# Two more turns for the DMA engines: q and k from the third batch on, A from the fourth, with a re-planned schedule

## The chip, the cores and the metric

The kernel runs on one core of a Trainium2 chip. The metric is the device time of one execution in microseconds (us). Before the change it was 260.49 us, the median of three runs (260.13 to 261.2). The profiled execution of it took 260.93 us, and the span of its instructions in the profile is 258.8 us; all times within the profile are counted from the start of that span.

The engines are named as the profile names them: PE is the matrix engine (PEld its weight loads), DVE the vector engine, ACT the scalar engine, POOL the general one (GpSimd), and SP the engine that does nothing here but issue DMAs.

## What is computed

The reference is Nystromformer attention over 8 batches of 8 heads, 576 positions and 64 features, followed by an MLP with a squared ReLU over the 4608 resulting rows of 512 features. Cut to what matters:

```python
q_lm = q.reshape(B, H, 32, 18, D).mean(axis=3)     # 32 landmarks, each a mean of 18 rows
k_lm = k.reshape(B, H, 32, 18, D).mean(axis=3)
A  = softmax(scale * q    @ k_lm.T)                # 576 x 32
Bm = softmax(scale * q_lm @ k_lm.T)                # 32 x 32
C  = softmax(scale * q_lm @ k.T)                   # 32 x 576
Z  = Bm.T / (norm1(Bm) * norminf(Bm) + 1e-6)
for _ in range(6):
    Z = 2 * Z - Z @ Bm @ Z                         # an approximate inverse
attn = A @ Z @ C @ v                               # per batch and head
h = attn_as_rows @ w_in                            # 4608 x 512 @ 512 x 2048
out = relu(h) ** 2 @ w_out                         # @ 2048 x 512
```

Inputs and output are float32; inside, the matrix engine works on bfloat16.

## The kernel before

**The work of one batch.** k, q and v come from device memory by DMAs that POOL issues (`load`, line 132; the first k by SP), cast to bfloat16 on the way except for that k. A batch's 576 rows lie as 4 blocks of 128 rows and a tail of 64 rows (`qkt` for k and q, `vt` for v). For the first three batches k and q are put into `stage`, which borrows a buffer of the MLP's; later ones use two buffers called `raw`. `prepare` (line 277) copies them on DVE into the order that the matmuls want (`nat`, line 280). From `nat`, PE forms the landmark means (`segment_means`, lines 341 and 351). The scores need k and q with the features on the partitions, so `nat` must be turned into `T` (`kT` and `qT`), and the tails into `tT`. Then come the landmark scores (line 371), the small Newton iteration for the inverse (line 413), the exponentials of A and C (`EA`, `EC`, lines 529 to 564), the sums and the scaling of A's rows into `an` (lines 571 to 583), and the turn of `an` into `AT`, with the 32 landmarks of four heads on the partitions.

The product of the rest is folded into the first weight matrix: `G` (line 806, cast on line 703) is Z C v times w_in. With it the MLP's first layer is a single product, `h` = AT x G (line 823), whose ReLU is taken by ACT (line 827) and squared by DVE into `gT` (line 828). The second layer is line 852: 36 output tiles of 128 rows, each of 16 matmuls of 512 columns, copied out on line 861 or 863 and sent off by a DMA (line 834 issues it). The last tile is made in two halves of 256 columns; the first goes out by DVE and SP, the second by ACT.

**Turning, on two engines.** A turn on PE (`transposed`, line 312; `transposed_tail`, line 322; `a_transposed`, line 596) multiplies by the identity into PSUM and is copied out by DVE or ACT (lines 662, 664, 685; 730 and 747 in the head). From batch `DMA_T` on, `prepare` instead lets SP issue a DMA that transposes (lines 285 and 286), and from batch `DMA_A` on `a_transposed` does the same (line 590). Before the change these are 3 and 4 (batches are counted from 0). `load_qk` makes the k and q loads of batch b wait for the DMA turns of batch b-1, and the k load also for the turns of A of batch b-2.

**The order of work.** For PE, DVE, ACT and SP it is written out by hand. `HEAD` is the order for the attention of batch 0. Then `PLANS[b]` interleaves, for each b, the 16 `h` and 16 squarings `s` of batch b's first layer, the attention steps of batch b+1 (a `+` behind a token puts it to batch b+2), and as many matmuls of the second layer as a number says, taken from one running generator over all output tiles. The tokens that matter here:

- `pk`, `pq`: prepare k or q; `tk0 tk1 tq0 tq1 tt`: turn on PE and copy out (they do nothing in a plan where DMAs turn, and are left out there)
- `mk`, `mq`, `lm`: means of k and of q, landmark scores; `ls ib if jo jl nu nn wt`: softmax and inverse
- `sk0 sk1 sq0 sq1 tl`: scores and exponentials against kT, qT and tT; `as ar at`: sums, rows and turn of A; `cv`: C v
- `gg0`, `gg1` (and `g:1` to `g:3` for batch 0): G; `w:n` in the head: n matmuls on zeros while PE waits for data

Every engine takes its instructions strictly in that order, so an instruction that waits holds up all behind it on its engine. POOL's DMAs run in the order of `LOADS` and then batch by batch (`load_next`).

Of the kernel before, what the change touches and what calls it, by code (L numbers as in the profile page):

```python
# [9 lines left out]
P = 128  # L10
# [5 lines left out]
F32 = mybir.dt.float32  # L16

B = 8
H = 8
# [5 lines left out]
DM = 512  # L25
# [3 lines left out]
TAIL = S - NC4 * P  # L29
HALF = S // 2  # L30
SCALE = 1.0 / 8.0
DMA_T = 3
DMA_A = 4
DMA_C = 9
COMPACT = 1
HEAD = (
    "w:16 ck tk1 tk0 ek0a w:1 ek1d w:1:256 cq0 w:1 mk cq1 w:1 tt mq et tq0 eq0a tq1 lm eq1d "
    "ls tl sum:0:4:5 sq1 ib sum:1:0:2 sk0 if w:1:256 sq0 w:1 sum:1:2:5 jo rec:1 sk1 "
    "sum:0:0:2 w:1:256 jo row:1:0:3 w:1:256 sum:0:2:4 w:1:256 jo cv:0 cv:1 rec:0 cr w:1 "
    "row:1:3:5 cba jo ct w:1:256 row:0:0:3 at:1 row:0:3:5 jl at:0 ea1a w:1 ea0d nu g:0 gf1a "  # L40
    "fv gf0d az gl0d w:1 gl1a"
)
LOADS = "v0 w10 w00 q1 w11 w01 o0 o1 v1 o2 o3"
PLANS = [
    (
        "pk h tt h g:1 s pq s tk1 h h tk0 tq1 h mk s s mq h s tq0 lm h h ls ib if sk0 s g:2 s jo "
        "g:3 tl h jo 2 sq0 s jo h s 1 as0 jl sq1 h h 1 ar0 nu sk1 s s h nn 1 h as1 1 s nu cv nn1 "
        "h s h wt 2 ar1 at0 gg1 s 1 s s 1 at1 2 gg0"
    ),
    (  # L50
        "6 h 1 s 5 h pk 2 h tt h 1 s 1 s 2 h 1 mk pq 1 mq tq0 1 h s 1 lm tq1 2 tl 1 s 1 h h 1 "
        "sq0 s 1 ls 1 ib if s 3 s 1 sq1 jo as1 h 3 tk0 2 pq+ 1 h jo h 1 tk1 1 s jo h 2 s 1 as0 1 "
        "jl 2 sk0 h 2 ar1 nu 3 s 1 nn sk1 1 ar0 1 h nu pk+ cv s 1 nn1 s 1 s 2 h 1 h wt 2 s at0 1 "
        "gg0 1 at1 1 s 2 gg1"
    ),
    (
        "mk 1 mq 1 h 3 lm 3 h s h ls sk1 2 ib 1 s h h s 1 s if s 2 tl 3 h 3 pk+ jo 1 sq1 3 h s s "
        "1 h sq0 jo s h as0 1 h jo 5 h s 1 h 1 as1 pq+ s jl 1 s 3 h h 1 sk0 nu 4 ar0 1 s ar1 s 4 "
        "cv nn 6 nu 3 at0 h 1 nn1 1 h s 4 wt 6 gg1 s 4 at1 s gg0 5"
    ),  # L60
    (
        "2 mk h 1 mq 3 h 1 lm 2 s 1 h 1 ls sk1 4 ib s 1 sq1 1 h 1 if pq+ 3 tl 1 jo 1 as1 3 pk+ 2 "
        "s h h 3 s s 1 s jo ar1 1 sq0 h 4 jo 4 s 2 jl as0 1 sk0 h 1 h s s 1 h 3 h nu s 1 h 1 s h "
        "nn cv ar0 h 3 nu s at0 1 at1 s h nn1 h s 3 wt s 4 s 3 gg0 5 gg1"
    ),
    (
        "mk 2 mq 9 lm 2 ls 1 h tl ib h 1 s 1 h 1 sq1 h 7 s 3 if h s 1 pq+ 1 h sq0 s s h jo 3 s s "
        "h as1 2 jo 6 h s 4 jo as0 1 h 1 pk+ 1 h 1 s jl 3 s 3 sk1 ar1 h 3 nu 3 sk0 1 ar0 1 s 1 "
        "nn at1 s 2 h nu h 1 nn1 cv h 1 s s 2 at0 s wt 1 h s 4 gg1 5 gg0"
    ),  # L70
    (
        "3 mk mq 6 lm 1 ls 2 ib 1 h s h sq0 2 h 3 if sq1 h 1 s s 2 jo h s pk+ 2 sk1 jo 1 h s 1 h "
        "s tl jo 4 s h 1 as0 h 1 ar0 4 jl 1 s sk0 h 1 h nu as1 s 4 h 2 s nn 2 at0 s 1 h nu ar1 3 "
        "s h cv nn1 s h s 1 at1 h 2 wt 1 s s 1 pq+ 3 gg0 7 gg1 3"
    ),
    (
        "mk h 1 s 7 mq h 1 h lm 2 h 1 sk1 4 s 2 ls ib if 3 s tl 1 s h 1 jo s h 1 s 1 sk0 jo 1 h "
        "1 cv h s 2 h 2 jo 1 sq0 1 h 2 as0 2 s 1 jl h s s h 1 ar0 s nu 4 sq1 h h 1 as1 4 nn 1 "
        "ar1 3 s nu 3 h 1 nn1 s 5 s s wt h 4 gg1 at1 s 5 gg0 at0 2"
    ),  # L80
    (
        "6 h 1 s 6 h 1 h s s 5 h 3 h 1 h s s 1 h s 2 h 4 s 3 h 2 h 1 s 1 s 3 h 2 h s 1 h 1 s 1 s "
        "1 h 1 h 1 s 8 h 1 s 4 s 5 s"
    ),
]

# [2 lines left out]
def kernel(  # L89
# [18 lines left out]
    psum = ctx.enter_context(tc.tile_pool(name="psum", bufs=1, space=bass.MemoryType.PSUM))  # L108

    w_in_bf = wpool.tile([P, DM // P, DFF], BF16, name="w_in_bf")  # L110
    w_out_bf = wpool.tile([P, NF, DM], BF16, name="w_out_bf")
# [44 lines left out]
    def load_qk(b: int, X: dict):  # L156

        X["qkt"] = loads.tile([P, H, D], BF16, tag="qkt", name="qkt")

        def tails():  # L160
            for src, r0 in ((k, k_row(b)), (q, q_row(b))):
                load(X["qkt"][r0:r0 + TAIL, :, :],
                     src[b, :, NC4 * P:S, :].rearrange("h p d -> p h d"))

        if b > 0:
            tails()
        for nm, src in (("k", k), ("q", q)):
            if b < 3:
                X[nm + "raw"] = staged(b, nm)
            else:  # L170
                X[nm + "raw"] = loads.tile([P, H, NC4, D], BF16, tag="raw", name="raw")
            parts = ((0, H // 2), (H // 2, H)) if b == 0 and nm == "q" else ((0, H),)
            for lo, hi in parts:
                one = load(
                    X[nm + "raw"][:, lo:hi, :, :],
                    src[b, lo:hi, 0:NC4 * P, :].rearrange("h (p c) d -> p h c d", c=NC4),
                    nc.sync if b == 0 and nm == "k" else nc.gpsimd)
                turns = [] if b == 0 else [loaded[b - 1].get(nm + "turn")]
                if b > 1 and nm == "k":
                    turns += loaded[b - 2].get("aturn", [])  # L180
                for turn in turns:
                    if turn is not None:
                        tc.add_manual_dep(
                            one.ins, turn.ins.name,
                            mybir.DependencyInfo(mybir.DependencyClass.Sync,
                                                 mybir.DependencyReason.DATA),
                            reason="behind the turning of the batch before")
            if b == 0 and nm == "k":
                tails()
# [43 lines left out]
    for i in range(2):  # L233
        ct = const.tile([P, 2, NC4 + 1, P], BF16, name="ct%d" % i)
# [62 lines left out]
    def attention(b: int, R: dict):  # L297
# [32 lines left out]
        def segment_means(ti, nm):  # L330
# [3 lines left out]
            means = both_means[ti]  # L334
            order = [(p, c) for p in range(NPAIR) for c in range(NC4 + first)]
            if first:
                order.sort(key=lambda x: (x[0] // 2, x[1] // 2, x) if nm == "q" else
                           (0, x[1] // 2, x))
            for n, (p, c) in enumerate(order):
                src = X[nm][:, c, 2 * p:2 * p + 2, :] if c < NC4 else X["qkt"][:, 2 * p:2 * p + 2, :]  # L340
# [3 lines left out]
                    rhs=seg[:, c + (ti if c == NC4 else 0), :],  # L344
# [151 lines left out]
        ct = cts[b % 2] if b >= DMA_C else None  # L496
# [212 lines left out]
        def head_step(token):  # L709
# [10 lines left out]
                st["qraw"] = natural(0, "q")  # L720
                X["tT"] = attn.tile([P, NPAIR, P], BF16, tag="tT", name="tT")
            elif name[:2] == "cq":
                lo = slice(4 * i, 4 * i + 4)
                dve(X["q"][:, :, lo, :], st["qraw"][:, :, lo, :])
            elif name[:2] in ("tk", "tq"):
                st["e" + name[1:]] = transposed(name[1], i)
# [103 lines left out]
    leaving = []  # L830
# [5 lines left out]
    def mlp_out(b, gT):  # L836

        b0 = b - b % 2
        for t in range(0, NC4) if b % 2 == 0 else range(NC4, 9):
            first, final = (b, t) == (0, 0), (b, t) == (B - 1, 8)  # L840
            if final:
                halves = [psum.tile([P, 2, DM], F32, tag="h", bufs=2, name="ops2")[:, 0, 0:DM // 2]
                          for i in range(2)]
            elif (b // 2 + t) % 2:
                halves = [ntile([P, DM], place=2)[:]]
            else:
                halves = [psum.tile([P, DM], F32, tag="o", bufs=1, name="ops")[:]]
            o_sb = mlp.tile([P, DM], F32, tag="o", bufs=3, name="o_sb")
            n = DM // len(halves)
            for i, ops in enumerate(halves):  # L850
                for f in range(NF):
                    nc.tensor.matmul(ops, lhsT=gT[:, f, t * P:t * P + P],  # L852
                                     rhs=w_out_bf[:, f, i * n:i * n + n],
                                     start=(f == 0), stop=(f == NF - 1))
                    if f == 2:
                        leave()
                    if f < NF - 1:
                        yield
                o_h = o_sb[:, i * n:i * n + n]
                if final and i == 0:  # L860
                    nc.vector.tensor_copy(o_h, ops)  # L861
                else:
                    nc.scalar.copy(o_h, ops)  # L863
                queue = nc.sync if final and i == 0 else nc.scalar
                if t == NC4:
                    for e in range(2):
                        r0 = (b0 + e) * S + NC4 * P
                        leaving.append(partial(queue.dma_start, out[r0:r0 + TAIL, :],
                                               o_h[64 * e:64 * e + TAIL, :]))
                else:  # L870
                    bb, c = (b0, t) if t < NC4 else (b0 + 1, t - NC4 - 1)
                    rows = out[bb * S:bb * S + NC4 * P, :].rearrange("(p c) n -> p c n", c=NC4)
                    leaving.append(partial(queue.dma_start, rows[:, c, i * n:i * n + n], o_h))
                if b == B - 1:
                    leave()
                yield
# [98 lines left out]
```

The softmax here doesn't subtract the row's maximum and nothing guards it: scores larger than these inputs give would overflow.

## Time and profile before

| | |
|---|---|
| Time, median of 3 runs | 260.49 us |
| Span in the profile | 258.8 us |
| Granted clock of PE | 0.998 of full speed |
| Moved by DMA | 35.96 MB, mean 139 GB/s |
| POOL's DMA queue q0 | 17.83 MB, 54.6% of the 16 engines' span |
| SP's queue q1 (first k, all turns) | 8.39 MB, 19.6% |
| ACT's queue q10 (outputs) | 9.31 MB, 10.4% |
| h matmuls (line 823), all 512 | 4 in 0.49 us of PE's stream |
| output matmuls (line 852), 560 of 512 columns | 16 in 3.45 us |

The page counts the busy time of each engine. On PE a matmul's duration reaches into the next one, so for PE the distance from one start to the next is read as well. The second part of the page cuts the span into 40 slices of 6.5 us and gives the busy share of each in tenths. The chain of waits follows the work that ended last back to what released it. DMA issues are listed with the median time from issue to landing.

### The profile page before, as it was taken

The page shows a single profiled execution, that of the slowest core. Times are in us where ns is not written, and L with a number is a line of the kernel's source. Part 1 is how long each engine was busy: PE and PEld are TensorE (multiplying, and loading weights), DVE is VectorE, ACT ScalarE, POOL GpSimd, SP SyncE. Part 2 cuts the span into 40 slices and gives each one's busy share as a digit, 9 for nine tenths or more (in the row PEclk, how much of TensorE's full clock was granted, in tenths as well). Part 3 has the DMA queues.
Part 4 walks back from the last instruction along what each step waited for, and adds up shares of the span by engine and source line. Part 5 has one row for each costly group of instructions (what it writes and reads, how often), then busy time and mean ns, then how long its engine had stood idle before and what let it go on. Part 6 is the DMA issues. An engine that isn't in the chain of part 4 may idle for free.

```text
span 258.8 us, 6890 instructions
## 1 busy us (share of the span) xinstructions
PE 250.1 (97%) x2832; PEld 150.7 (58%) x2832; DVE 174.9 (68%) x483; ACT 156.7 (61%) x275; POOL 45.5 (18%) x70
## 2 busy tenths in 40 slices
PE   7888899999999999999999999999999999999994
PEld 2655756576656655666646655566556654655453
DVE  5796899678987784588764877688857687243000
ACT  2657897677577754666756555586557655566110
POOL 8934335120024013200042002500000000000000
PEclk9999999999999999999999999999999999999999
DMA  8999999996669999959159988999351113111222
GB/s 190 180 199 204 207 200 196 193 209 122 137 104 179 209 181 168 171 113 188 35 98 199 197 196 124 148 223 176 100 123 43 43 41 91 43 42 72 52 81 81
DMA packets 75167, 35.96 MB, mean 139 GB/s; under 512 B 42752, under 2 KB 69632, under 8 KB 75136
## 3 DMA queue, kind: packets, MB, share of 16 engines
q0 software_dynamic: 39808, 17.83, 54.6%
q1 hardware_dynamic: 30080, 8.39, 19.6%
q10 hardware_dynamic: 5248, 9.31, 10.4%
q8 instruction: 22, 0.36, 0.5%
q14 instruction: 9, 0.07, 0.1%
HBM read 36.70 MB, written 9.44 MB: 178 GB/s over the span
## 4 chain that ended last, share of the span: by engine, by line
PE 86%; DMA 6%; POOL 4%; DVE 2%; issue 0%; ACT 0%; POOLq 0%; DVEq 0%
PE ops L852 26%; PE h L823 23%; PE n L852 23%; DMA stage<-in_q_dram 6%; PE g L806 3%; PE n L529 3%; PE n L341 2%; PE n L413 1%; PE n L614 1%; POOL qkt L134 1%; PE n L312 1%; PE n L629 1%; POOL stage L134 1%; PE n L596 1%; PE n L557 1%; POOL seg L205 1%
## 5 line engine op out<-in xcount | busy, mean ns | idle before, releaser
L827 ACT ACTIVATE r<-h 128x576 bf16<-128x576 f32 x128 | 81.9, 651 | 42.8 <-PE h L823 32.8
L852 PE MATMUL ops<-w_out_bf,gT 128*128 128x512 bf16 (+1 forms) x320 | 82.5, 368 | 0.0
L852 PEld LDWEIGHTS <-gT 128*128 128x128 bf16 x592 | 53.1, 97 | 39.9 <-issue 4.2
L852 PE MATMUL n<-w_out_bf,gT 128*128 128x512 bf16 x272 | 72.1, 379 | 0.0
L823 PE MATMUL h<-AT,G 128*128 128x288 bf16 x448 | 71.5, 286 | 0.0
L828 DVE TENSOR_TENSOR gT<-r 128x576 bf16<-128x576 bf16 x128 | 55.2, 449 | 19.4 <-ACT r L827 19.0
L823 PEld LDWEIGHTS <-G 128*128 128x128 bf16 x512 | 47.3, 98 | 22.3 <-DVE AZ L796 0.3
L703 DVE CAST G<-g 128x1024 bf16<-128x1024 f32 x14 | 17.1, 1222 | 6.6 <-PE g L806 6.6
L134 POOL DMA_DIRECT2D raw<-in_k_dram x5 | 4.4, 888 | 80.3 <-DMA AT<-an 23.5
L703 ACT CAST G<-g 128x1024 bf16<-128x1024 f32 x14 | 14.2, 1012 | 7.1 <-PE g L806 7.1
L863 ACT COPY o_sb<-ops 128x512 f32<-128x512 f32 (+1 forms) x19 | 10.9, 573 | 12.1 <-PE ops L852 9.0
L863 ACT COPY o_sb<-n 128x512 f32<-128x512 f32 x17 | 10.0, 587 | 8.5 <-PE n L852 8.5
L529 PEld LDWEIGHTS <-T 128*128 128x128 bf16 x256 | 11.4, 98 | 4.4 <-ACT T L730 0.5
L571 DVE TENSOR_REDUCE ra<-EA 128x20 f32<-128x640 f32 (+3 forms) x19 | 13.3, 698 | 0.6 <-ACT EA L534 0.6
L583 DVE TENSOR_TENSOR an<-EA,rra 128x640 bf16<-128x640 f32 (+2 forms) x18 | 13.1, 734 | 0.0
L529 PE MATMUL n<-bd,T 128*128 128x64 bf16 x256 | 12.8, 193 | 0.3 <-ACT T L730 0.3
L534 ACT ACTIVATE EC<-n 128x512 bf16<-128x512 f32 x16 | 9.6, 599 | 5.8 <-PE n L529 5.7
L534 ACT ACTIVATE EA<-n 128x512 f32<-128x512 f32 x16 | 9.6, 599 | 2.7 <-PE n L529 2.6
L294 PE MATMUL idle<-bd 128*128 128x512 bf16 (+1 forms) x29 | 9.3, 434 | 1.5 <-DVE bd L117 1.5
L823 PE MATMUL h<-AZ,G 128*128 128x288 bf16 x64 | 9.8, 286 | 0.1
L341 PEld LDWEIGHTS <-nat 128*128 128x128 bf16 x256 | 8.2, 96 | 2.7 <-issue 0.5
L861 DVE COPY o_sb<-ops 128x256 f32<-128x256 f32 x1 | 0.4, 425 | 13.6 <-PE ops L852 13.6
(144 smaller groups left out, 278.9 us busy)
## 6 DMA issues: line engine op xcount, KB each, us to landing
out_dram<-o_sb ACTq DMA_DIRECT2D x31, 256.0 KB, 2.9
vm<-in_v_dram POOLq DMA_DIRECT2D x8, 512.0 KB, 12.0
raw<-in_k_dram POOLq DMA_DIRECT2D x5, 512.0 KB, 6.7
raw<-in_q_dram POOLq DMA_DIRECT2D x5, 512.0 KB, 9.6
w_in_bf<-in_moe_w_in_dram POOLq DMA_DIRECT2D x4, 512.0 KB, 12.3
w_out_bf<-in_moe_w_out_dram POOLq DMA_DIRECT2D x4, 512.0 KB, 17.0
out_dram<-o_sb ACTq DMA_DIRECT2D x9, 128.0 KB, 3.5
stage<-in_k_dram SPq DMA_DIRECT2D x1, 1024.0 KB
```

Of the source, the lines that this page charges most:

```text
L134: d = queue.dma_start(dst, src)
L341: nc.tensor.matmul(means[:, ti, p, :], lhsT=src.rearrange("p h d -> p (h d)"), rhs=seg[:, c + (ti if c == NC4 else 0), :], start=(n == 0 a ...
L529: nc.tensor.matmul(sc[:, c, j, :, :], lhsT=X[nm + "T"][:, c, p, :], rhs=BD[:, 1 if nm == "q" else 0, p, 0:64], start=True, stop=True)
L534: nc.scalar.activation(dst, sc.rearrange("p c j i m -> p c (j i m)"), AF.Exp, scale=SCALE)
L571: nc.vector.reduce_sum(ra[:, quads, lo:hi, :], EA[:, quads, lo:hi, :].rearrange("p q c (h m) -> p q c h m", m=M), axis=AX.X)
L583: on.tensor_tensor(an[:, i, lo:hi, :].rearrange("p c (h m) -> p c h m", m=M), EA[:, i, lo:hi, :].rearrange("p c (h m) -> p c h m", m=M), r ...
L703: (act, dve)[n % 2](G[:, :, n * 512:n * 512 + 512], gg[:])
L823: nc.tensor.matmul(h[:, j, 0:HALF], lhsT=G[:, qd, f * P:(f + 1) * P], rhs=AT[:, qd, a0 + j * HALF:a0 + (j + 1) * HALF], start=(qd == 0), s ...
L827: nc.scalar.activation(r.rearrange("p (j t) -> p j t", j=2), h[:, :, 0:HALF], AF.Relu)
L828: return lambda: nc.vector.tensor_tensor(gT[:, f, o:o + S], r[:], r[:], ALU.mult)
L852: nc.tensor.matmul(ops, lhsT=gT[:, f, t * P:t * P + P], rhs=w_out_bf[:, f, i * n:i * n + n], start=(f == 0), stop=(f == NF - 1))
L863: nc.scalar.copy(o_h, ops)
```

## The change

`DMA_T` goes from 3 to 2 and `DMA_A` from 4 to 3: the third batch's k and q with their tails, and the fourth batch's A, are turned by DMAs instead of PE. It is meant to take this work from PE and the copies from DVE and ACT.

The first batch's q is loaded as 6 heads and 2 heads, not as 4 and 4, so that what is left to cast after the last landing is less; the order of its mean matmuls follows that. Of the weights, the half `w00` is loaded ahead of the first v instead of behind it.

The last output tile is cut in 384 and 128 columns, not in two halves, so that the copy and the DMA behind the last matmul are smaller.

`HEAD` and all of `PLANS` are written anew for this. The number of h, squarings and output matmuls in all is the same; 7 output matmuls more than before are in plan 0 (19, not 12) and 12 more in plan 1 (79, not 67), so that fewer are left for the end. In plan 0 the two casts for batch 2 (`pk+`, `pq+`) now stand at the end; before, they stood in plan 1.

```diff
-DMA_T = 3
-DMA_A = 4
+DMA_T = 2
+DMA_A = 3
 HEAD = (
-    "w:16 ck tk1 tk0 ek0a w:1 ek1d w:1:256 cq0 w:1 mk cq1 w:1 tt mq et tq0 eq0a tq1 lm eq1d "
...
+    "w:16 ck tk0 w:1:256 w:1 ek0a cq0 w:1 w:1 cq1 tk1 ek1a mk tt mq tq1 lm tq0 et eq0a eq1d "
...
-LOADS = "v0 w10 w00 q1 w11 w01 o0 o1 v1 o2 o3"
+LOADS = "w00 v0 w10 q1 w11 w01 o0 o1 v1 o2 o3"
 PLANS = [
     (
-        "pk h tt h g:1 s pq s tk1 h h tk0 tq1 h mk s s mq h s tq0 lm h h ls ib if sk0 s g:2 s jo "
-        "g:3 tl h jo 2 sq0 s jo h s 1 as0 jl sq1 h h 1 ar0 nu sk1 s s h nn 1 h as1 1 s nu cv nn1 "
-        "h s h wt 2 ar1 at0 gg1 s 1 s s 1 at1 2 gg0"
+        "h h pk tt h s s g:1 tk0 h h mk pq s s mq tq0 lm ls tq1 h s ib h if tk1 h jo g:2 jo s "
+        "sq1 g:3 jo s h s tl 1 jl as1 s h h nu 1 sq0 1 s h ar1 nn 1 sk1 1 s h sk0 as0 s nu h h s "
+        "nn1 cv s 1 h wt at1 2 ar0 gg1 s 1 s 1 at0 1 gg0 6 pk+ 2 pq+"
     ),
     (
-        "6 h 1 s 5 h pk 2 h tt h 1 s 1 s 2 h 1 mk pq 1 mq tq0 1 h s 1 lm tq1 2 tl 1 s 1 h h 1 "
-        "sq0 s 1 ls 1 ib if s 3 s 1 sq1 jo as1 h 3 tk0 2 pq+ 1 h jo h 1 tk1 1 s jo h 2 s 1 as0 1 "
-        "jl 2 sk0 h 2 ar1 nu 3 s 1 nn sk1 1 ar0 1 h nu pk+ cv s 1 nn1 s 1 s 2 h 1 h wt 2 s at0 1 "
-        "gg0 1 at1 1 s 2 gg1"
+        "6 h 3 s h 1 h 1 mk s 5 h 1 mq 1 h 2 lm s s ls h 1 h 1 s h ib 2 if tl s 2 s s h 2 jo s 1 "
+        "h 4 h jo 1 h 1 s 2 jo 1 sk1 s h 3 jl 1 h s 1 s nu 1 sk0 h 4 s nn cv nu h 1 s 1 s 1 sq1 "
+        "nn1 3 as1 4 ar1 sq0 pk+ 2 wt 2 as0 4 ar0 at1 2 gg0 7 at0 4 gg1 pq+"
     ),
...
-            parts = ((0, H // 2), (H // 2, H)) if b == 0 and nm == "q" else ((0, H),)
+            parts = ((0, 6), (6, H)) if b == 0 and nm == "q" else ((0, H),)
...
-                order.sort(key=lambda x: (x[0] // 2, x[1] // 2, x) if nm == "q" else
+                order.sort(key=lambda x: (x[0] // 3, x[1] // 2, x) if nm == "q" else
...
-                lo = slice(4 * i, 4 * i + 4)
+                lo = slice(6, H) if i else slice(0, 6)
...
-                halves = [psum.tile([P, 2, DM], F32, tag="h", bufs=2, name="ops2")[:, 0, 0:DM // 2]
-                          for i in range(2)]
+                halves = [psum.tile([P, 2, DM], F32, tag="h", bufs=2, name="ops2")[:, 0, 0:w]
+                          for w in (3 * DM // 4, DM // 4)]
```

The other six plans are reordered in the same way.

## The prediction

> **What bounds the kernel now.** I read the page's engine totals and slices, then busy time by stretch, then TensorE's (PE's) timeline around the work the change moves, then the DMA landings.
>
> ```profile
> PE 250.1 (97%) x2832; PEld 150.7 (58%) x2832; DVE 174.9 (68%) x483; ACT 156.7 (61%) x275; POOL 45.5 (18%) x70
> ...
> PE   7888899999999999999999999999999999999994
> ...
> DMA  8999999996669999959159988999351113111222
> ```
>
> PE is below 9 only in the first five slices (6.5 us each) and the last; the DMA engines are full for nine slices, to about 58 us. Matmuls overlap, so 97% alone proves little. The stretches say more (from:to, us, PE busy, matmuls, clock, DMA share, over 1 where packets overlap, and GB/s):
>
> ```profile
> 22.00:34.00 12.00, 10.55 (x165) 1.00 1.23 207
> 34.00:46.00 12.00, 12.00 (x219) 1.00 1.46 197
> 46.00:76.00 30.00, 30.00 (x370) 1.00 1.05 160
> 76.00:105.00 29.00, 29.00 (x319) 1.00 1.20 173
> ```
>
> PE idles 1.45 us between 22 and 34 us, where batch 0's MLP runs, and not at all later. The start-to-start distances agree: after 50 us they sit at the spacing of their kind (16 output matmuls in 3.45 us, 0.216 each; four h matmuls in 0.49; eight transposes in 0.45). So after 34 us the end is set by the sum of PE's work: what leaves PE there leaves the time, and what delays PE there adds to it. Before 34 us PE waits for data; the chain of waits shows for what:
>
> ```profile
> 11.75 14.59 DMA stage<-in_q_dram
> 26.36 0.70 DVE nat L280
> 27.11 0.62 PE n L312 x8
> ```
>
> Batch 1's q lands at 26.34, 14.59 us after its issue. PE's timeline (start, us, ..., count) shows the work that is to leave, each with the next start behind it:
>
> ```profile
> 53.82 0.61 PE L312 MATMUL n<-ident_bf,nat 128*128 128x128 bf16 x8
> 54.27 0.38 PE L852 MATMUL ops<-w_out_bf,gT 128*128 128x512 bf16 x1
> ...
> 97.96 0.44 PE L596 MATMUL n<-ident_bf,an 128*128 128x128 bf16 x5
> 98.24 0.65 PE L823 MATMUL h<-AT,G 128*128 128x288 bf16 x4
> ```
>
> The duration column (0.61) is longer than the place taken (53.82 to 54.27, 0.45), as matmuls overlap. The DMA issues (name, queue, count, median us to landing):
>
> ```profile
> T<-nat SPq DMA_TRANSPOSE x10, 5.3
> AT<-an SPq DMA_TRANSPOSE x8, 3.9
> ...
> tT<-qkt SPq DMA_TRANSPOSE x5, 2.8
> ```
>
> **What the Trainium skill says.** "Trainium Kernel Development and Optimization" (Performance Expectations) calls matmul busy time a bad measure, as matmuls are pipelined; the trace agrees (0.38 us long, 0.216 apart), hence the distances. "VectorE: DVE Perf Modes" (The three transpose paths) gives 390 ns for a 128x128 transpose on TensorE and 1309 ns on the DMA; in this trace a PE transpose takes 0.055 us of PE's stream, and a DMA turn of 16 blocks lands in 5.3, 0.33 a block. So the DMA is slower and pays only by leaving PE alone. "TensorE: Matmul & The Clock Gate" (PE-mode transpose) says the result goes to PSUM and needs a copy out; the trace has them, 0.69 us on VectorE (DVE), 1.01 on ScalarE (ACT). "DMA: Bandwidth & Descriptors" (Issuing engines are not separate DMA queues) says DMAs of all issuers interleave on the same 16 engines; the trace agrees: the T turns land in 4.4 to 8.8 us, the 8.8 at 85 us with loads and outputs in flight.
>
> **The change part by part.** *Off PE.* Batch 2's k and q: 4 groups of 8 transposes, at 53.82, 55.29, 61.03 and 63.38, of 0.45, 0.45, 0.44, 0.44 = 1.78 us. Its tails: 4 at 50.41, 0.22. Batch 3's A: 2 groups of 5 (from 97.96), 0.28 each, 0.56. All lie after 34 us, so they count in full: **-2.56 us**. Their copies (T 0.69 and 1.01 twice each, tT 0.42, AT 0.45 and 0.64) leave DVE and ACT, 68% and 61% busy: 0 on the path.
>
> *Onto the DMA.* One tail turn and two T turns near 46 to 60 us, two AT turns near 96. Queue q1 moved 8.39 MB in 19.6% of 258.8 us, 6.0 us per MB; so the first three (0.13 + 2 x 0.52 MB) cost about 7 us of the 16 engines, in a stretch where they are full to 58. Estimated positions in the new plans, with each token at its measured place in PE's stream (h 0.49, one output matmul 0.216, g pair 0.56, scores 0.23, means 0.40 and 0.51), plan 0 starting at 22.0 as before and losing the same 1.45 to waits: plan 1 starts at 45.7. The casts `pk+` and `pq+` stand at the end of plan 0, at 45.3 and 45.7. Their data was issued at 33.2 and 35.7; staged loads land in 13.2 (median) to 14.6, so at 46.4 to 47.8 and 48.9 to 50.3; with 0.69 for a cast they are done by 48.5 and 51.0. PE wants them for `mk` at 49.5 and `mq` at 51.7: 0.7 us of room at worst. Queued behind the waiting DVE are the squares; r has three buffers and h two, so PE notices at the sixth h, at 53.2, a good us after the casts are done. The turns then go out at 48.5 and 51.0 and land, at 5.3 to 8.8, by 57.3 and 59.8; wanted for `sk1` at 61.2 and `sq1` at 67.3. `tl` wants the tail at 55.8; issued near 46, landed by 52. All hidden: **0**.
>
> *Held loads.* With DMA_T = 2 batch 3's k and q wait for batch 2's turns: not issued at 44.6 and 45.5 but near 57 and 60. Raw loads take 6.7 and 9.6 (medians): 64 and 70. `pk+` and `pq+` for batch 3 stand near 69 and 75. Behind them on GpSimd's queue is batch 4's k (75.9 before), due again only after batch 3's k turn, near 76. Batch 5's loads now wait also for batch 3's AT turns: issued near 96 and 97, landed by 102 (3.9, 4.7 at most), while the first h that reads AT stands near 107, and batch 5's casts come after 118: **0**.
>
> *The head and plan 0.* q in 6 and 2 heads leaves a shorter cast behind the last landing (4 heads took 0.49; a quarter of q about 0.25); v behind a weight load arrives some 2.5 us later, near 15.5, against its first use at 16.4. But batch 1's q bounds what follows, so the head itself: 0. After that landing the old plan runs `tq1`, an h, `mk`, `mq`, an h, `tq0` and only then `lm` (27.11 to 29.97); the new one does `mk` ahead of it and then `mq tq0 lm`: about 28.2. The latency chain of batch 1 starts 1.8 us sooner, with five h before the landing, not four. What this can win is between 0 and the 1.45 idle; I take half: **-0.7 us**.
>
> *Last tile.*
>
> ```profile
> 255.23 0.37 ACT L863 COPY o_sb<-ops 128x256 f32<-128x256 f32 x1 [2.91 <-PE ops L852]
> 255.64 0.34 ACTq L834 DMA_DIRECT2D out_dram<-o_sb  x1
> ```
>
> PE: 32 x 0.109 = 3.49 becomes 16 x 0.162 + 16 x 0.055 = 3.47. The last copy shrinks to 128 columns, about 0.27 (the 128x128 ACT copies), and its transfer by 64 KB (256 KB lands in 2.3, 128 KB in 1.85): some 0.1 each, **-0.2 us**. The 384-column part ends 0.9 before PE's end, and its copy (0.42 x 1.5) hides there.
>
> Sum: 260.49 - 2.56 - 0.7 - 0.2 = **257.0 us**.
>
> **The rivals.**
> - *Only the PE work counts.* The early idle is bounded by landings and stays: 260.49 - 2.76 = 257.7. For: the chain passes through 14.59 us of DMA. Against: half of the idle comes after the landing, inside batch 1's small steps.
> - *A landing takes the transposes' place.* Batch 2's q is wanted 0.7 us after its latest expected cast; if loads land 3 us later than before, PE waits about 2.3 at `mq` and little is kept: 260.0. For: full DMA engines. Against: the loads ahead of it are the same; only a 0.13 MB turn gets in.
> - *The turns chain up, slower.* Full engines make the three turns land one after another, at 8.8 each: q's at about 67, and batch 3's k, issued at 58.6 and taking 13, lands at 72, not before its cast at 69. PE loses 2.3 us there, and as much once more where batch 3's own turn comes late: 260.49 - 2.76 + 4.6 = 262.3. For: only five turns are added, but two thirds of their bytes fall into the fullest stretch. Against: holding the loads back empties the load queue just as the turns need it.
>
> **How the numbers follow.** The forecast 0.52, only PE work 0.25, a landing 0.11, chained turns 0.12. The first two are faster by over 0.5% (below 259.2), the third mostly no change, the fourth slower. The range runs from 255.6 (all of the 1.45 and half a microsecond of the head won) to 260.2, which holds most of the third case and leaves out the fourth: about 0.82. Faster 0.79, same 0.09, slower 0.12.
>
> **What would show it.** Right: PE full from about 33 us on in the stretches, L312 with 64 matmuls and L596 with 30, twelve T turns, and no wait of PE, or of the first scores of batch 2, on a T turn; plan 1's `mq` not ended by a q landing. Wrong: PE idle near 50 to 52, 61 or 107, DVE's cast waiting for a load near 69, or T turns near 50 landing later than 9 us after issue.

## The result, and the profile after

The kernel after took 258.1 us (median of 4 runs, 257.53 to 258.48), the kernel before beside it 260.76. The ratio is 0.990, with a 95% interval of 0.987 to 0.993: **2.7 us faster**. The forecast was 257.0, in a range of 255.6 to 260.2. Ratios here leave out disturbed runs and medians do not, so where the two disagree, the ratio times 260.76 is given as the time.

The profiled run of the kernel after took 257.53 us, with a span of 255.7, against 258.8 before: 3.1 less. Its engine totals and slices:

```profile
PE 247.7 (97%) x2784; PEld 146.8 (57%) x2784; DVE 173.1 (68%) x478; ACT 154.2 (60%) x273; POOL 45.7 (18%) x70
...
PE   7888999999999999999999999999999999999994
...
DMA  7999999999998999999949799999469013211122
```

PE has 48 matmuls fewer (46 of the transposes and two fillers `w`), and its slices are at 9 from the fifth on, one slice sooner than before. The DMA engines are now full, but for two slices, through the first 20 (to 128 us), where before slices at 5, 6 and even 1 began with the tenth. The stretches (from:to, us, PE busy, matmuls, clock, DMA share, GB/s):

```profile
22.00:34.00 12.00, 11.17 (x181) 1.00 1.23 207
34.00:46.00 12.00, 12.00 (x208) 1.00 1.46 197
46.00:76.00 30.00, 30.00 (x318) 1.00 1.25 167
76.00:105.00 29.00, 29.00 (x319) 1.00 1.22 168
```

PE's idle time between 22 and 34 us fell from 1.45 to 0.83. After 34 us there is still none, so in this run every added turn was hidden. The groups of transposes (line, tiles, count | busy, mean ns | idle before), those of before and, below them, those of after:

```profile
L596 PE MATMUL n<-ident_bf,an 128*128 128x128 bf16 x40 | 3.7, 220 | 0.0
L312 PE MATMUL n<-ident_bf,nat 128*128 128x128 bf16 x64 | 4.9, 219 | 1.1 <-DVE tT L664 0.6 <-DVE nat L280 0.4
L312 PE MATMUL tps<-ident_bf,nat 128*128 128x128 bf16 x32 | 2.1, 219 | 0.6 <-ACT nat L718 0.6
```

```profile
L594 PE MATMUL n<-ident_bf,an 128*128 128x128 bf16 x30 | 2.7, 220 | 0.0
L310 PE MATMUL n<-ident_bf,nat 128*128 128x128 bf16 x32 | 2.5, 219 | 0.2 <-DVE T L660 0.2
L310 PE MATMUL tps<-ident_bf,nat 128*128 128x128 bf16 x32 | 2.4, 219 | 0.0
```

Lines of the kernel after stand 2 lower than before (L310 was L312). A's turns fell from 40 to 30, k's and q's from 96 to 64, and those of the tails from 12 to 8. The turns went to SP. Its timeline (start, us, queue) for batch 2, and below it what `T` needed from issue to landing, of these two turns and then of all twelve:

```profile
44.20 1.38 SPq L283 DMA_TRANSPOSE tT<-qkt  x1
47.55 12.19 SPq L284 DMA_TRANSPOSE T<-nat  x2
...
DMA to landing us min/median/max: 9.3/11.0/12.7
```

```profile
DMA to landing us min/median/max: 4.8/7.1/12.7
```

k's turn was issued at 47.55 and landed at 60.20, q's at 52.97 and 62.27. PE reads them here:

```profile
62.46 0.40 PE L527 MATMUL n<-bd,T 128*128 128x64 bf16 x8
...
68.66 0.40 PE L527 MATMUL n<-bd,T 128*128 128x64 bf16 x8
```

So k's turn had 2.3 us to spare and q's 6.4. The held loads show on POOL's timeline; the bracket is the idle time before an instruction and what ended it:

```profile
60.73 0.89 POOL L132 DMA_DIRECT2D raw<-in_k_dram  x1 [16.60 <-DMA T<-nat]
62.80 0.88 POOL L132 DMA_DIRECT2D raw<-in_q_dram  x1 [1.18 <-DMA T<-nat]
```

Batch 3's loads go out only once batch 2's turns have landed. Whatever stands behind a held load on POOL's queue waits with it. So batch 3's v waits behind batch 4's q, which is held for batch 3's turn. Its issue on POOL's timeline, and its first reader on PE's:

```profile
88.00 0.88 POOL L132 DMA_DIRECT2D raw<-in_q_dram  x1 [7.57 <-DMA T<-nat]
...
89.74 0.71 POOL L132 DMA_DIRECT2D vt<-in_v_dram  x1
```

```profile
100.67 0.20 PE L612 MATMUL n<-vt,ect 128*32 128x64 bf16 x4
```

This tail of v took 10.8 us to land, so it was there at 100.54, only 0.13 us ahead of its reader. Before the change it was issued at 78.56, landed 12.0 us later and was read at 95.36, with 4.8 to spare.

The end, on ACT's timeline:

```profile
252.07 0.27 ACT L863 COPY o_sb<-ops 128x128 f32<-128x128 f32 x1 [2.91 <-PE ops L852]
252.36 0.34 ACTq L832 DMA_DIRECT2D out_dram<-o_sb  x1
```

From the start of the last copy to the end of the span it is 3.64 us; before, it was 3.59 (255.23 to 258.82).

### The profile page after: what moved, and what is told of

Same layout as the page of the kernel before. It is cut to its first block, busy times and chain, and to the rows that moved or that the text cites. A ratio compares the mean times of both kernels' runs of the same rounds, so it can differ in the third digit from the quotient of the medians.

```text
span 255.7 us, 6802 instructions
## 1 busy us (share of the span) xinstructions
PE 247.7 (97%) x2784; PEld 146.8 (57%) x2784; DVE 173.1 (68%) x478; ACT 154.2 (60%) x273; POOL 45.7 (18%) x70
## 3 DMA queue, kind: packets, MB, share of 16 engines
q10 hardware_dynamic: 5248, 9.24, 11.5%
## 4 chain that ended last, share of the span: by engine, by line
PE 90%; DVE 4%; DMA 2%; POOL 1%; issue 1%; ACT 0%; POOLq 0%
PE ops L852 26%; PE h L821 24%; PE n L852 23%; PE g L804 3%; PE n L527 3%; DMA stage<-in_q_dram 2%; PE n L411 2%; PE n L339 2%; PE n L612 1%; PE n L627 1%; PE n L594 1%; PE n L555 1%; POOL qkt L132 1%; DVE nat L278 1%; DVE T L660 1%
## 5 line engine op out<-in xcount | busy, mean ns | idle before, releaser
L852 PE MATMUL ops<-w_out_bf,gT 128*128 128x512 bf16 (+2 forms) x320 | 82.2, 368 | 0.0
L852 PEld LDWEIGHTS <-gT 128*128 128x128 bf16 x592 | 52.4, 97 | 40.6 <-issue 4.6
L821 PE MATMUL h<-AT,G 128*128 128x288 bf16 x448 | 70.6, 286 | 0.0
L821 PEld LDWEIGHTS <-G 128*128 128x128 bf16 x512 | 48.0, 98 | 24.1 <-DVE AZ L794 0.6
L863 ACT COPY o_sb<-ops 128x512 f32<-128x512 f32 (+1 forms) x19 | 10.8, 570 | 10.4 <-PE ops L852 7.3
L527 PE MATMUL n<-bd,T 128*128 128x64 bf16 x256 | 12.7, 193 | 0.0
L416 DVE SCALAR_TENSOR_TENSOR EY<-EY,n 128x128 bf16<-128x128 bf16 x25 | 7.0, 278 | 5.4 <-PE n L411 5.4
L861 DVE COPY o_sb<-ops 128x384 f32<-128x384 f32 x1 | 0.6, 558 | 13.6 <-PE ops L852 13.6
## 6 DMA issues: line engine op xcount, KB each, us to landing
vm<-in_v_dram POOLq DMA_DIRECT2D x8, 512.0 KB, 10.8
```

The source lines that it names most:

```text
L527: nc.tensor.matmul(sc[:, c, j, :, :], lhsT=X[nm + "T"][:, c, p, :], rhs=BD[:, 1 if nm == "q" else 0, p, 0:64], start=True, stop=True)
L821: nc.tensor.matmul(h[:, j, 0:HALF], lhsT=G[:, qd, f * P:(f + 1) * P], rhs=AT[:, qd, a0 + j * HALF:a0 + (j + 1) * HALF], start=(qd == 0), s ...
L852: nc.tensor.matmul(ops, lhsT=gT[:, f, t * P:t * P + P], rhs=w_out_bf[:, f, cols], start=(f == 0), stop=(f == NF - 1))
```

## The experiments

Each starts from the kernel after unless it says otherwise. Times to compare are 258.1 (after) and 260.8 (before).

**One part at a time.** The old head, loads and 4+4 heads on the new plans:

```diff
-LOADS = "w00 v0 w10 q1 w11 w01 o0 o1 v1 o2 o3"
+LOADS = "v0 w10 w00 q1 w11 w01 o0 o1 v1 o2 o3"
-            parts = ((0, 6), (6, H)) if b == 0 and nm == "q" else ((0, H),)
+            parts = ((0, H // 2), (H // 2, H)) if b == 0 and nm == "q" else ((0, H),)
...
```

> The changed kernel with the head of the kernel before: its HEAD, its order of loads, q in 4 and 4 heads. Plans and turns stay. Theory (the head is worth nothing, as batch 1's q bounds what follows; the first h began at 22.0 before and 22.1 after): 258.1 within 0.4, PE idle between 22 and 34 us about as in the changed kernel, 0.8. Rival (the head brought the 0.6 us of early idle): 258.7 or more.

It took 257.8 us, ratio 0.989 (0.986 to 0.992). The first h stands at 22.24 us against 22.12 with the new head and 21.99 in the kernel before. No worth of the new head shows.

The last tile in halves again:

```diff
-                          for w in (3 * DM // 4, DM // 4)]
+                          for w in (DM // 2, DM // 2)]
```

> The changed kernel with the last tile in two halves of 256 columns again. The prediction gave the cut 0.2 us: 258.3, with the stretch from the start of the last ACT copy to the end of the span longer by 0.2 than the 3.65 us of the changed kernel. Rival (the two last transfers now lie on top of each other, so the smaller one lands no sooner): 258.1, and that stretch is 3.6 as it was before, 3.59.

The ratio is 0.992 (0.989 to 0.995), or 258.7, an interval that overlaps that of the kernel after. From the last copy to the end it took 3.74 us against 3.64, so by these two traces the cut is worth 0.1. The times lie 0.6 apart and can neither show that nor exclude more.

The landmark scores of batch 1 behind the turn again:

```diff
-mq tq0 lm ls tq1 h s ib
+mq tq0 tq1 h s lm ls h ib
```

> The kernel after, with one edit in plan 0: the landmark scores and their softmax of batch 1 stand behind the second turn of q and an h again, not ahead of them. Theory (the earlier landmark scores start batch 1's chain of small steps sooner, and that is what cut PE's idle time between 22 and 34 us by 0.62): that idle comes back, 258.5 to 258.8 us, with over 1.2 us of PE idle in that stretch. Rival (the idle fell because five h, not four, stand ahead of q's landing; the place of the landmark scores is worth nothing): 258.1 us, idle of some 0.8 as in the kernel after.

The ratio is 0.997 (0.994 to 1.001), or 260.1: 2.0 us lost by moving one small step, where 0.4 to 0.7 were forecast. The stretches and PE's waits in the first of them:

```profile
22.00:34.00 12.00, 9.74 (x148) 1.00 1.22 206
34.00:46.00 12.00, 11.91 (x229) 1.00 1.46 197
```

```profile
PE n L310 <- DVE T L660: 0.8, 1, 0.8
PE n L426 <- ACT Eb L372: 0.7, 1, 0.7
PE h L821 <- DVE AZ L794: 0.3, 1, 0.3
PE n L426 <- DVE BB L381: 0.3, 1, 0.3
```

Idle time before 34 us rose from 0.83 to 2.26: PE now waits for the copy of the first turn (L660), and then for the exponential and the softmax behind the late landmark scores (L372, L381). The means that follow q's landing start at 26.22 us, against 26.03, so the load was hardly later. Of the 1.43 more, 0.22 is a later first h (22.34). Another 0.25 comes with the edit itself, which puts two turns next to each other: 0.80 at L310, where the kernel after waits 0.37 for the landmarks and 0.18 there. The other 0.97 is the late chain. Some 0.5 of the 2.0 us is not accounted for.

The early idle was thus mostly a matter of order, but landings have a part. In the 12 us from the first h, PE idles 1.45 before the change and 0.71 after it; in eight other runs with this plan 0 and the full clock there it is 0.73 to 1.30. In the two with the most, PE waits 0.5 and 0.6 for the cast of batch 1's q, and the cast 0.4 and 0.5 for the landing.

**What a PE transpose costs.** Turning on PE again, in the new plans, with the five old tokens put back in plan 1:

```diff
-DMA_T = 2
-DMA_A = 3
+DMA_T = 3
+DMA_A = 4
-... h ib 2 if tl s 2 s s h 2 jo s 1 h 4 h jo ... jl 1 h s ... nn cv ...
+... h ib tt 2 if tl s 2 s s h tk0 2 jo s 1 h tk1 4 h jo ... jl tq0 1 h s ... nn tq1 cv ...
```

> The changed kernel with its head, its plans and its last tile, but batch 2's k, q and tails and batch 3's A are turned on PE again (thresholds 3 and 4; the five turning steps put back into plan 1). Theory (PE's work after 34 us sets the end): the 2.56 us of transposes come back in full, so 258.1 + 2.6 = 260.7 us, and L310 and L594 show 96 and 40 matmuls again. Rival 1 (the new order of steps brought the gain): stays within 0.5 us of 258.1. Rival 2 (the copies on DVE and ACT, not the transposes, were what cost): more than 2.6 us slower than the changed kernel, with PE idle behind a copy in plan 1.

It took 272.2 us (268.8 to 274.3), ratio 1.046 (1.041 to 1.052), where 260.7 was forecast. PE's timeline shows waits at the tail's copy and, at 107 and 109 us, at v loads:

```profile
59.39 0.40 PE L555 MATMUL n<-bd,tT 128*128 128x128 bf16 x4 [1.19 <-DVE tT L662]
...
107.08 0.30 PE L612 MATMUL n<-vm,EC 128*32 128x64 bf16 x16 [0.54 <-DMA vm<-in_v_dram]
108.91 0.21 PE L612 MATMUL n<-vt,ect 128*32 128x64 bf16 x4 [1.53 <-DMA vt<-in_v_dram]
```

That is no clean price: waits for a copy and for loads are mixed into it. Adding transposes and leaving the rest alone was the second attempt, 48 of them in plans 2 to 6, each group like this:

```diff
+            elif kind == "xx":
+                tps = ntile([P, 2, NPAIR, P], BF16, place=1)
+                for j in range(2 * NPAIR):
+                    nc.tensor.transpose(tps[:, j // NPAIR, j % NPAIR, :], ident_bf[:], ident_bf[:])
```

> The changed kernel with 48 more transposes on PE (of the identity, into PSUM, read by nobody), in six groups of 8 in plans 2 to 6, so in the stretch where PE never idles; no copy, no wait, no DMA. Theory (there PE's work is the time): + 48 x 0.0555 = 2.66, so 260.8 us. Rival (PE has hidden room there, the page's 97% or not, and the gain came from elsewhere): less than half of that.

The ratio is 1.020 (1.014 to 1.025), or 265.8, three times the forecast loss. Again DMAs came late, here for batch 5:

```profile
150.92 0.41 PE L527 MATMUL n<-bd,T 128*128 128x64 bf16 x8 [1.54 <-DMA T<-nat]
163.54 0.21 PE L612 MATMUL n<-vt,ect 128*32 128x64 bf16 x4 [1.00 <-DMA vt<-in_v_dram]
```

The same turn took 6.9 us in the kernel after and had 2.2 to spare; here it took 11.5 and held back q's and v's loads behind it. An output and a load of k had gone out shortly ahead of it in both, k's 2.5 us ahead there and 1.6 here; what made the turn slow is not shown. The two waits are 2.5 us; with 2.7 for the transposes, some 2.5 of the loss stays open. The third attempt put the 48 into the last plan, which has no load or turn left:

```diff
-        "9 h 3 h 1 s 3 s h h 2 h s 3 h 5 s 2 ...
+        "9 xx h 3 h 1 s 3 s h h 2 xx h s 3 h 5 xx s 2 ...
```

> The kernel after, with 48 transposes by the identity (6 groups of 8, results unused) put into the last plan, where no input load and no DMA turn is left that could slip. Theory (each PE transpose costs its place in PE's stream, 0.055 us, and the rest of what the earlier 48 cost, 8 us for 2.6, was loads and turns that slipped): 258.1 + 48 x 0.055 = 260.8 us, and PE free of waits in the last plan. Rival (a group costs more in itself, as the 0.6 to 0.7 us between its neighbours in the earlier run suggests: it waits for its PSUM tile, or breaks the stream): 6 x 0.65 = 3.9, 262 us. Rival (the tail of the kernel is set by outputs and copies, PE's work hides): 258.1 to 259.

It took 260.7 us (ratio 1.001, 0.999 to 1.003): 2.6 us for 48, or **0.054 us each** (the interval allows 2.4 to 3.4). PE's timeline:

```profile
223.67 0.61 PE L927 MATMUL n<-ident_bf 128*128 128x128 bf16 x8
224.12 0.65 PE L821 MATMUL h<-AT,G 128*128 128x288 bf16 x4
```

0.45 us for eight, as in the kernel before. The price of the prediction holds, where no DMA depends on the place.

The profiled execution took 264.4 us, and it shows something else. Up to 200 us its instructions are those of the kernel after, but batch 3's v came too late:

```profile
101.63 0.30 PE L612 MATMUL n<-vm,EC 128*32 128x64 bf16 x16 [0.29 <-DMA vm<-in_v_dram]
103.38 0.21 PE L612 MATMUL n<-vt,ect 128*32 128x64 bf16 x4 [1.45 <-DMA vt<-in_v_dram]
```

The 0.13 us of room can thus be missed without any edit ahead of it. The v waits near 107 and 109 us in the run with PE's turns back can therefore not be put down to its edit alone.

**Why the turns fit.** The new thresholds in the plans of before, less the five turning tokens that they make idle:

```diff
-DMA_T = 3
-DMA_A = 4
+DMA_T = 2
+DMA_A = 3
```

> The kernel before with the thresholds at 2 and 3 alone; the five turning steps are left out of plan 1, all else, order included, is as before. Theory: a turn takes 9 to 13 us while the loads run (9.3 and 12.7 in the changed kernel), and here q is cast near 52.5 and wanted by its first scores near 58, k's near 50.5 and 66: q lands at 62 to 65, so PE waits 4 to 7 us and the 2.56 saved are lost: 262 to 265 us, slower than before. Rival (turns are hidden anyway, the new plans are not needed for them): 260.7 - 2.6 = 258.1, as the changed kernel.

The ratio is 1.055 (1.046 to 1.063), or 275.0: the thresholds alone lose 14 us, where 262 to 265 us were forecast. The wait of 10.5 below is the most of it; 1.8 us are lost already at the first h (23.79), with a clock of 0.51 from 18.5 to 25.5 us, ahead of any turn that the thresholds move. PE's timeline, then POOL's:

```profile
58.48 0.38 PE L852 MATMUL ops<-w_out_bf,gT 128*128 128x512 bf16 x1
69.36 0.61 PE L529 MATMUL n<-bd,T 128*128 128x64 bf16 x8 [10.50 <-DMA T<-nat]
```

```profile
45.13 0.89 POOL L134 DMA_DIRECT2D raw<-in_k_dram  x1
46.01 0.89 POOL L134 DMA_DIRECT2D raw<-in_q_dram  x1
```

Batch 3's loads went out at 45 and 46 us, not held at all. The code says why: `load_qk(3)` runs at the head of plan 1 and waits only for a turn that is already written down. In the old plans batch 2's `pk` and `pq` come after it; with `pk+` and `pq+` at the end of plan 0 they come before. By the code, then, the move of these two tokens is what makes the hold work. What the hold is worth shows when it alone is taken away:

```diff
-                turns = [] if b == 0 else [loaded[b - 1].get(nm + "turn")]
+                turns = [] if b in (0, 3) else [loaded[b - 1].get(nm + "turn")]
```

> The changed kernel, but batch 3's k and q loads do not wait for batch 2's turns, so that they go out near 44.5 and 45.5 us as in the kernel before. Theory (holding them back is what lets the turns land in time): 1.05 MB more, written as bfloat16 from twice that read, stand beside the turns; k's turn lands near 65 instead of 60.2 and PE, which wants it at 62.5, waits 2 to 3 us: about 260.5. Rival (the turns' pace is set by their own packets): they land as before, at 60 and 62, and the time stays 258.1.

The ratio is 1.011 (1.004 to 1.018), or 263.6, 5.5 us worse, where 2.4 was forecast. The waits on PE's timeline in the profiled execution, of 266.8 us, and the landing times of `T`:

```profile
65.27 0.41 PE L527 MATMUL n<-bd,T 128*128 128x64 bf16 x8 [1.53 <-DMA T<-nat]
73.57 0.41 PE L527 MATMUL n<-bd,T 128*128 128x64 bf16 x8 [1.93 <-DMA T<-nat]
```

```profile
DMA to landing us min/median/max: 4.3/6.8/17.8
```

With two raw loads ahead of them, batch 2's turns took 16.6 and 17.8 us, not 12.7 and 9.3. The two waits make 3.5 us. Waits for batch 3's v of 1.1 and 1.3 follow, near 107 us; v has so little room that these need not come from the edit. The last test of the room reads kT sooner:

```diff
-... jo s 1 h 4 h jo 1 h 1 s 2 jo 1 sk1 s h 3 ...
+... jo s 1 sk1 h 4 h jo 1 h 1 s 2 jo 1 s h 3 ...
```

> The kernel after, with one token of plan 1 moved: the first scores against batch 2's kT (sk1) stand 3.5 us earlier in PE's order, at 58.93 us, ahead of an h and four output matmuls. In the kernel after kT lands at 60.20 and is read at 62.46. Theory (nothing but that room of 2.3 us kept the late turns off PE's path): PE waits some 60.2 - 58.9 = 1.3 us there, and the time is 258.1 + 1.3 = 259.4 us; if a stretch at half clock follows the wait, as it did in the runs with waits before, up to 1.7 more, 261.1. Rival (the turn lands when it is needed, or other instructions fill in): 258.1 us and no wait of PE on T.

The ratio is 0.996 (0.993 to 0.999), or 259.7: 1.6 us lost, 1.3 forecast. In its profiled run PE ran 1.8 us later from the head on, and so waited less:

```profile
60.55 0.38 PE L852 MATMUL ops<-w_out_bf,gT 128*128 128x512 bf16 x1
61.31 0.41 PE L527 MATMUL n<-bd,T 128*128 128x64 bf16 x8 [0.39 <-DMA T<-nat]
```

The turn landed at 61.27 and the scores started at 61.31, so they ran as soon as it was there. The later start is not the edit's: the clock was 0.52 from 13.0 to 16.4 us, in the head. The loss agrees with a wait of 1.3, but the one trace shows only 0.39 of it.

**Where the thresholds end.** A of batch 3 back on PE (`DMA_A = 4`), and A of batch 2 on the DMA as well (`DMA_A = 2`):

```diff
-DMA_A = 3
+DMA_A = 4
```

> The changed kernel with the threshold for A at 4 again, so that batch 3's A is turned by 10 transposes on PE in plan 2 and copied out by DVE and ACT; nothing else moves. Theory (PE's work after 34 us counts in full): + 10 x 0.056 = 0.56 us, so 258.7, with batch 5's k load going out earlier than the 107.6 us of the changed kernel. Rival (what waits around the two A turns, batch 5's loads above all, had a price of its own): not slower, or even faster than 258.1.

```diff
-DMA_A = 3
+DMA_A = 2
```

> The changed kernel with one step further, the threshold for A at 2: batch 2's A too is turned by DMAs, near 73 and 76 us. Theory by the sum alone: - 0.56 us, so 257.5. But the second half of A is ready near 74.5 and would be read by the first h of plan 2 near 78.7, while a turn took 5 to 8.5 us in the changed kernel: it lands at 80 to 83, PE waits 1 to 4 us, and batch 4's k load now waits for it as well: 259 to 262. The second is what I expect; the first if the room is larger than that.

The first: ratio 0.994 (0.992 to 0.997), or 259.3; 1.2 us lost where 0.56 of PE's work came back, though the interval, 258.6 to 260.0, does not exclude 0.56. The profiled execution, of 262.9 us, has waits of 1.8 on batch 5's T and 0.9 on its vt, as in the run with transposes in plans 2 to 6. The second: 1.012 (1.005 to 1.019), or 263.9, where 259 to 262 were forecast; PE's timeline shows the turn arriving late:

```profile
82.02 1.14 PE L821 MATMUL h<-AT,G 128*128 128x288 bf16 x4 [4.16 <-DMA AT<-an]
```

In these plans batch 2's A is turned right ahead of its first reader; its turns were issued at 76.0 and 77.4 and landed at 81.6 and 82.0. Batch 3's were issued at 98.1 and 100.2, landed by 107.0, and were read at 109.41.

## Why the prediction was right, point by point

- **Off PE, -2.56: right.** 48 late transposes cost 2.6 us, and PE after the change is as full after 34 us as before it.
- **Early idle, -0.7: right in cause; the size was half of what could be had, a guess, and came out well by luck.** It fell by 0.62, and by less in some other runs with this plan 0. The landmark scores stand at 28.14, where the prediction had 28.2; moving them back cost 2.0 us. The rival that only PE's work counts (257.7) lies nearer to the median than the forecast (0.4 against 1.1); what speaks against its reason is the idle time and that run.
- **Head, 0: right.** The first h is 0.13 later, and the old head is as fast within the intervals.
- **Last tile, -0.2: wrong.** This is the term that was mis-sized. The smaller copy gained 0.10 (0.37 to 0.27), but the last DMA gained nothing by its size: the end came 3.37 us behind the 128-column copy (3.64 less 0.27), and the same 3.37 behind the 256-column one in the run with halves (3.74 less 0.37); before the change it was 3.22. The estimate compared transfers of 256 and 128 KB and carried their difference on to 64 KB.
- **Turns and casts, 0: right in effect, wrong in a step.** "Land, at 5.3 to 8.8" became 12.7 and 9.3. The prediction took the range of before, when no turn ran in the fullest stretch. Three things absorbed it: the casts were earlier (46.77 and 49.75 on DVE), the scores later (62.46, not 61.2), and loads were held. The first two were not planned for and are luck. So the sign named as "wrong", a turn near 50 us landing more than 9 us after issue, came true without the cost; the time to the reader should have been named, not the time to land. The rival of chained turns had the durations about right; it took q's turn to start when k's had landed, and they overlapped. The rival of a late landing of batch 2's q did not come about: its cast began at 49.75, when it had landed, within the 48.9 to 50.3 of the forecast, and PE did not wait for it.
- **Held loads, 0: right in effect, with two things missed.** Loads issued at 60.73 and 62.80 landed by 71.88, where 64 and 70 were forecast, and nobody waited. The prediction priced the hold at nothing and named its use only against a rival; it is the means, and without it the gain turns into a loss. And the prediction left out batch 3's v, which stands behind the held q of batch 4 and so goes out 11 us later than before (89.74, not 78.56). That it came 0.13 us ahead of its reader is luck; in the profiled execution with late transposes it came too late.
- **A's turns, 0: right, with less room.** Landed by 107.0, not 102, and read at 109.41, not 107.

The terms -2.56 - 0.62 + 0.05 make the 3.1 by which the span fell; the head's 0.13 lies within the 0.62, as the stretch began at 22.00. The median gained 2.7, 0.8 less than the forecast; 0.25 of that is the last tile, 0.1 the idle, and the rest is less than the interval, 257.3 to 258.9, can tell apart. The 19 output matmuls that moved into plans 0 and 1 had no run of their own; PE is full from 34 us on either way.

## What to carry to other kernels

Work that leaves a full engine is worth its place in the stream, but only as far as the new carrier arrives before its reader: write down, for every moved transfer, when it is issued, when it lands in that traffic, and when it is read. A transfer's time must be taken from a stretch as busy as the one it moves to. Where a transfer is tight, what is kept out of its way (here the next batch's loads) can be worth more than the transfer itself. But ask what stands behind a held load on its queue (here v), for it is held too. And the order in which the program is written can silently decide whether a hold exists.

## What the runs showed of the hardware that was not expected

In one run, that with loads not held, a turn of 16 blocks took 4.3 us at best and 17.8 behind two loads of k and q: a factor of four for the same transfer.

After PE had stood still for 4.2 us in the run with `DMA_A = 2`, it ran at half clock for the next stretch (from:to, us, PE busy, matmuls, clock, DMA share, GB/s):

```profile
78.00:81.40 3.40, 0.00 (x0) 1.00 1.28 211
81.40:84.80 3.40, 2.56 (x8) 0.50 0.93 192
84.80:88.00 3.20, 3.20 (x41) 1.00 1.24 140
```

That makes a wait dearer than its length: PE worked at half clock from 82.02 to 84.8, by estimate 1.4 us more, half of these 2.8. "TensorE: Matmul & The Clock Gate" (Part 1: The HAM clock gate) of the Trainium skill describes a half rate after an idle window of some 3.4 us and a return after as long a busy one; this trace agrees. Other traces differ from it: PE need not idle for so long. In the profiled execution with late transposes, the 3.4 us with the two waits for v were half busy, and half clock followed:

```profile
101.30:104.70 3.40, 1.66 (x55) 1.00 1.48 200
104.70:108.10 3.40, 3.40 (x25) 0.50 1.56 122
```

In the run with loads not held the clock was 0.51 for 3.4 us after the waits of 1.1 and 1.3. Yet the waits of 0.5 and 1.5 in the run with PE's turns back, and the 1.8 with batch 3's A on PE, kept the full clock. What decides between them is not shown.
